# Set attention and a gated feed-forward layer on one core: the product sums of three groups in one PSUM buffer, and the small work around the first attention rearranged

## The chip, the cores and the metric

The kernel runs on one core of one Trainium2 chip. The metric is the device time of one execution in microseconds. Three executions of the kernel before gave 1244.42, 1245.16 and 1248.59 us, so the median is 1245.16 us. A measurement of this kernel can tell a change of about 0.3% (some 3.7 us) from no change.

## What is computed

Four batches of 12608 rows of 128 numbers are attended twice through 32 inducing rows, and every row of the result then goes through a feed-forward layer of width 1024 with a softmax gate and a layer norm:

```python
h  = mab(I, x)            # first attention: 32 inducing rows look at all rows of x
y  = mab(x, h)            # second attention: every row of x looks at the 32 rows h
hh = y @ w_in             # 128 -> 1024
solu = hh * softmax(hh)
ln = (solu - mean) / sqrt(var + 1e-6) * g_ln
out = ln @ w_out          # 1024 -> 128
```

`mab(q, kv)` is softmax(q kv^T / sqrt(128)) kv with the row maximum taken off first.

## The kernel before

**Tiles.** A batch is 99 slots of 128 rows (the last one has 64), in 25 groups of four slots. The kernel folds the second attention into the first matmul of the layer: for each slot, `main` multiplies the slot's 32 attention weights (tile `aT`) by `hs`, a 32 x 1024 product of `h` and `w_in`, in eight small matmuls (L1009). These write one of the four PSUM buffers `h0` to `h3`, each of two PSUM banks. There are 396 such slots.

**One slot's way** (`soft`): VectorE scales and takes the minimum (L1050), ScalarE exponentiates with a sum (L1061), GpSimd multiplies the two (L1065), ScalarE squares with a sum (L1076), VectorE transposes in blocks of 32 (L1089). When the four slots of a group are transposed, `products` starts two streams, w = 0 and w = 1. Each stream accumulates 32 steps in a PSUM buffer of its own (L1132, output 128 x 2 x 129: 128 columns and the sum). `evacuate` copies the buffer to SBUF (L1155), on VectorE or ScalarE. After five groups, `finish` works out mean and variance in a chain of small ScalarE and GpSimd instructions (L1177 to L1191), GpSimd scales each group's rows (L1198), and the rows are stored. There are 100 groups and 20 calls of `finish`.

**Row groups of TensorE.** All these matmuls contract over 32 rows, so four can run side by side, in the four 32-row strips of the array. A stream uses two strips (w = 0 the lower two, w = 1 the upper two), and so does a slot's matmul or a transpose of 32 rows. The helper `beats` writes the order: in one beat it emits a pair of matmuls for each stream that has work, or a pair of a slot's or a transpose's matmuls and a pair of the other stream. A beat with two pairs is called full in this document, one with a single pair half.

**First attention** (`p1`). For batches 1 to 3 it runs beside the layer of the batch before, in groups of up to 16 slots (seven per batch): x is loaded by DMA, transposed on TensorE (L583), copied (L593), stored transposed in DRAM for the second attention, scored against the inducing rows (L643), and the maximum per row of scores is taken on VectorE (L659). Scores lie in four quarters of the partitions, so the four partial maxima have to become one: VectorE spreads them (L663), one small matmul with `fold2` brings them together (L668), VectorE takes the maximum with the running one (L677) and scales it (L684). Then comes the exponential (L694), a transpose (L714), a matmul that gathers the weighted rows of x (L725) in a second visit to a PSUM buffer, and the update of the running sum (L741). Batch 0 does the same in the start of the kernel with PSUM buffers of its own (`early`). `combine` closes a batch (L767 to L793), and `p2` makes the weights of the second attention (L833 to L910).

**What sets the order.** A planner written in Python lists the instructions: each has an engine, a cost, what it comes after, and a priority, and each engine's list is fixed before the launch. The numbers at the top of the file (`EAGER`, `P1_STEP`, `PR_*`, `SLACK`, `WINDOW_TILES`, `MINE`) set priorities and windows. On the chip each engine takes its list in that order and waits on semaphores. `PAIR[w]` lets a stream have one group at a time, `TURN` (of `MINE` tokens) limits slots between L1009 and L1050, and `H` holds the four PSUM buffers. `HN` and `EU` are the buffers of L1050 and L1061.

Of the kernel before, what the change touches and what calls it, by code (L numbers as in the profile page):

```python
# [19 lines left out]
P = 128  # L20
C = 128
# [12 lines left out]
EAGER = 300  # L34
SWITCH = 400

# [19 lines left out]
HN_MORE = 4  # L56
# [6 lines left out]
P1_STEP = 10.5  # L63
# [5 lines left out]
PR_G2 = 8  # L69
PR_HN = -4  # L70
PR_MU = -4
PR_SQ = 4
PR_TU = 12
RUSH = -100.0
SLACK = {"PE": 0, "ACT": 200, "DVE": 100, "POOL": 100, "SP": 0}
SPARE = 150
WARM = 32
WINDOW_TILES = 3
MINE = 2
OP_FIRST = -30  # L80
WOUT = -8
WIN = -18.5
# [8 lines left out]
DMA_LAG = 1800  # L91
# [159 lines left out]
def set_attention_then_solu_kernel(ctx: ExitStack, tc: tile.TileContext, x, inducing, w_in, w_out, g_ln, out):  # L251
# [67 lines left out]
    EW = Lock()  # L319
    ST = Lock([  # L320
# [9 lines left out]
    SM = Lock([small(i, mloc=1, mdiag=4, junk=4, nb=1, fac=1, ls=1, rl=1) for i in range(4)])  # L330
# [200 lines left out]
    turned = [Event() for _ in range(NP[0])]  # L531

    def p1(b, k):
# [9 lines left out]
        halves = [(0, GS), (GS, n)] if early and not k and n > GS else [(0, n)]  # L543
        for c0, c1 in halves:
            for nbytes, fn in move(b, s0 + c0, c1 - c0, xn[:, c0:, :], False):
                d = yield dma(nbytes, fn, rel)
                xd.append((d, c0))
# [21 lines left out]
        def by_rows(ways):  # L569
# [4 lines left out]
            def turn():  # L574
                w = min(ways, key=lambda w: (load(w) > 0, w))
# [9 lines left out]
                beats(-(-n // 2), (1 - w,), two)  # L585

# [35 lines left out]
        def store():  # L622
            def go():
                nc.sync.dma_start(xT_dram[b][:, s0 * P : (s0 + n) * P], xT[:, :n, :].rearrange("p s t -> p (s t)"))

            d = yield dma(n * P * C * 4, go, ready)
            plan.set(xd_done[(b, k)], d)
            plan.set(stored, d)
# [5 lines left out]
        if not early:  # L634
            (eT, ew), erel = yield lew
# [11 lines left out]
        d = yield Op("PE", (0 if early else SWITCH) + n * 60, scores, ready, rel, ind_ready.after)  # L647
# [9 lines left out]
        for lo, hi, nn in parts:  # L657
            d = yield Op(
                "DVE", 411, lambda: nc.vector.tensor_reduce(out=v["mloc"][lo:hi], in_=sc[lo:hi, : nn * M], op=ALU.max, axis=AX.X), dsc  # L659
            )  # L660
        d = yield Op(
            "DVE", 131,
            lambda: nc.vector.tensor_scalar(  # L663
                out=v["mdiag"], in0=quarter, scalar1=v["mloc"], scalar2=None, op0=ALU.mult, op1=ALU.max, accum_out=v["nb"]
            ),
            d,
        )
        d = yield Op("PE", (80 if early else SWITCH) + 110, lambda: nc.tensor.matmul(mq, lhsT=fold2, rhs=v["mdiag"], start=True, stop=True), d)  # L668
# [6 lines left out]
        d = yield Op(  # L675
            "DVE", 122,
            lambda: nc.vector.tensor_scalar(  # L677
                out=v["junk"], in0=mq, scalar1=(-3.0e38 if first else mold), scalar2=None, op0=ALU.max, op1=ALU.max, accum_out=mnew
            ),
            d, prev,  # L680
        )
        plan.set(chain[b][k + 1], d)
        dm = d = yield Op(
            "DVE", 70, lambda: nc.vector.tensor_scalar(out=v["nb"], in0=mnew, scalar1=-scale, scalar2=None, op0=ALU.mult), d  # L684
        )
        df = None
        if early:
            (eT, ew), erel = yield lew
# [9 lines left out]
        de = d = yield Op("ACT", (130 + 35 * n) * len(parts) + (0 if first else 190), exps, dm, erel)  # L698
# [15 lines left out]
        d = yield Op("DVE", 435, lambda: nc.vector.transpose(out=ew[:, :n, :].rearrange("p s m -> p (s m)"), in_=eT[:, : n * M]), d)  # L714
        nq = min(4, n)
        rel = None
        if not early:
            give(lpb, big, de)
            big, rel = yield lpb
        pooled = big[:, 512 - C : 512]  # L720

        def gather():
# [6 lines left out]
        dp = yield Op("PE", 74 * n, gather, d, rel)  # L729
# [20 lines left out]
        give(lpb, big, da)  # L750
# [9 lines left out]
    def combine(b):  # L760
# [11 lines left out]
        d = yield Op("DVE", 200, lambda: nc.vector.tensor_scalar(out=accn, in0=acc, scalar1=rl, scalar2=None, op0=ALU.mult), d, prev)  # L772
# [33 lines left out]
    def p2(b, j):  # L806
# [4 lines left out]
        for k, (g0, gn) in enumerate(p1_groups[b]):  # L811
# [4 lines left out]
        d = yield dma(  # L816
            n * P * C * 4,
            lambda: nc.sync.dma_start(xT[:, :n, :].rearrange("p s t -> p (s t)"), xT_dram[b][:, s0 * P : (s0 + n) * P]),
            rel, prev,
        )  # L820
# [38 lines left out]
        def turned_rows():  # L859
# [4 lines left out]
            def turn():  # L864
                w = min(ways, key=lambda w: (load(w) > 0, w))
# [11 lines left out]
                beats(-(-pairs // 2), (1 - w,), two)  # L877

# [40 lines left out]
    stream = [dict(j=JB, emit=None, ready=0.0, close=None) for _ in range(2)]  # L919
    flow = {"idle": Event(), "left": 2 * NB * NG, "prio": 0.0}  # L920

    def load(w):
        p = stream[w]
        return JB - p["j"] if p["j"] < JB and p["ready"] <= plan.now + EAGER else 0

    def beats(count, pairs=(0, 1), also=None):

        for i in range(count):
            if also:
                also(i)  # L930
            went = False
            for w in pairs:
                p = stream[w]
                if p["j"] < JB and p["ready"] <= plan.now + i * BEAT + EAGER:
                    p["emit"](2 * w, p["j"])
                    p["emit"](2 * w + 1, p["j"])
                    p["j"] += 1
                    went = True
            if not (went or also):
                return i  # L940
        return count
# [374 lines left out]
```

## Time and profile before

| what | value |
|---|---|
| median of three executions | 1245.16 us |
| the profiled execution: its own time | 1244.09 us |
| its span, first to last instruction | 1242.3 us |
| TensorE matmul busy | 1196.1 us (96%) |
| VectorE, ScalarE, GpSimd busy | 1092.8, 1085.6, 1087.8 us |
| mean granted TensorE clock | 0.979 |
| DMA | 113.61 MB, mean 91 GB/s |

Durations below come from this one profiled execution. Matmuls overlap each other, so a busy TensorE is not a full TensorE. A float32 matmul stands in the records twice: 12800 product matmuls are 25600 records. The column after the engines in a table of stages is the granted clock of TensorE, 1.00 being full speed.

### The profile page before, as it was taken

To read this page: it belongs to the slowest core of one execution; us is meant where nothing else is said; L and a number is where in the kernel's file an instruction comes from. 1 tells how busy PE (TensorE), PEld (TensorE's weight loads), DVE (VectorE), ACT (ScalarE), POOL (GpSimd) and SP (SyncE) were. 2 spreads that over 40 slices of the span, in tenths; PEclk is the share of its full clock that TensorE was granted. 3 is DMA by queue.
4 is the path that set the end of the run, shared out by engine and by line. 5 is a ranking of instruction groups with operands and counts; after the bars stand their busy time and mean duration, and the time that the engine had idled before them with its cause. 6 is when DMAs were issued, how large, how long until landed. Compare 5 with 4: busy or idle time off the path is not lost. (4 is left out here: it accounts for less than half of the span.)

```text
span 1242.3 us, 77962 instructions
## 1 busy us (share of the span) xinstructions
PE 1196.1 (96%) x35557; PEld 1112.9 (90%) x35557; DVE 1092.8 (88%) x1684; ACT 1085.6 (87%) x2152; POOL 1087.8 (88%) x638
## 2 busy tenths in 40 slices
PE   9999999999999989999999999999999999999995
PEld 7679999999998988998999899999899999999995
DVE  5689999999897989899988889989899999898982
ACT  5489998999897979898889889999888999998983
POOL 3478898988987878989898898989898999998996
PEclk9969999999999999999999999999999999989998
DMA  9663243321234233331223333523220212112013
GB/s 355 234 166 111 72 135 90 101 68 38 81 90 130 82 102 110 94 104 50 73 56 108 103 112 101 158 57 110 63 54 16 73 48 61 47 19 48 6 47 85
DMA packets 152908, 113.61 MB, mean 91 GB/s; under 512 B 76257, under 2 KB 132609, under 8 KB 148097
## 3 DMA queue, kind: packets, MB, share of 16 engines
q1 hardware_dynamic: 152576, 108.62, 29.2%
q8 instruction: 278, 4.55, 1.6%
q14 instruction: 54, 0.43, 0.1%
HBM read 54.30 MB, written 52.18 MB: 86 GB/s over the span
## 5 line engine op out<-in xcount | busy, mean ns | idle before, releaser
L1132 PE MATMUL h<-wc,vt 32*128 32x129 f32 (+1 forms) x25600 | 1030.4, 275 | 22.4 <-issue 13.7
L1132 PEld LDWEIGHTS h<-wc,vt 32*128 32x128 f32 (+1 forms) x25600 | 992.7, 186 | 60.6 <-issue 38.6
L1065 POOL TENSOR_TENSOR eu<-spare,eu 128x1024 f32<-128x1024 f32 x227 | 535.7, 2376 | 45.3 <-ACT eu L1061 45.0
L1089 DVE STREAM_TRANSPOSE vt<-eu 128x1024 f32<-128x1024 f32 x396 | 481.6, 1230 | 13.5 <-POOL eu L1065 12.9
L1076 ACT ACTIVATE sq<-eu 128x1024 bf16<-128x1024 f32 x396 | 416.7, 1052 | 47.5 <-POOL eu L1065 37.0
L1009 PE MATMUL h<-hs,aT 32*128 32x128 f32 x6336 | 435.2, 276 | 4.1 <-ACT aT L889 1.7
L1065 POOL TENSOR_TENSOR eu<-hn,eu 128x1024 f32<-128x1024 f32 x169 | 399.7, 2377 | 38.9 <-ACT eu L1061 38.7
L1009 PEld LDWEIGHTS h<-hs,aT 32*128 32x128 f32 x6336 | 392.2, 189 | 23.2 <-issue 6.7
L1050 DVE TENSOR_SCALAR_CACHE_REDUCE spare<-h,rn 128x1024 f32<-128x1024 f32 x227 | 285.8, 1265 | 40.4 <-PE h L1009 23.8
L1061 ACT ACTIVATE eu<-spare,nm 128x1024 f32<-128x1024 f32 x227 | 259.1, 1142 | 10.3 <-DVE spare L1050 7.8
L1050 DVE TENSOR_SCALAR_CACHE_REDUCE hn<-h,rn 128x1024 f32<-128x1024 f32 x169 | 212.8, 1264 | 29.9 <-PE h L1009 17.0
L1061 ACT ACTIVATE eu<-hn,nm 128x1024 f32<-128x1024 f32 x169 | 192.9, 1142 | 7.4 <-DVE hn L1050 4.8
L1198 POOL TENSOR_TENSOR spare<-spare,fin 128x512 f32<-128x512 f32 x100 | 101.2, 1044 | 1.4
L1076 ACT ACTIVATION_READ_ACCUMULATOR sq<-eu 128x1 f32 x396 | 74.8, 189 | 0.0
L1155 ACT COPY spare<-h 128x258 f32<-128x258 f32 (+1 forms) x127 | 45.7, 364 | 29.4 <-PE h L1132 28.2
L583 PE MATMUL h<-ident,xn 32*128 32x32 f32 x1188 | 54.1, 225 | 0.3 <-issue 0.3
L583 PEld LDWEIGHTS h<-ident,xn 32*128 32x128 f32 x1188 | 50.4, 136 | 0.7 <-issue 0.5
L593 ACT COPY xT<-h 128x1024 f32<-128x1024 f32 (+2 forms) x42 | 37.8, 901 | 10.1 <-PE h L583 9.8
L1155 DVE COPY spare<-h 128x258 f32<-128x258 f32 (+1 forms) x73 | 30.2, 416 | 18.4 <-PE h L1132 18.0
L1061 ACT ACTIVATION_READ_ACCUMULATOR eu<-spare,nm 128x1 f32 x227 | 43.0, 190 | 0.0
L875 PE MATMUL h<-ident,a 32*128 32x32 f32 (+1 forms) x800 | 34.2, 221 | 1.4 <-ACT a L852 1.1
L889 ACT COPY aT<-h 128x512 f32<-128x512 f32 (+3 forms) x66 | 30.2, 472 | 5.6 <-PE h L875 5.5
(154 smaller groups left out, 655.2 us busy)
## 6 DMA issues: line engine op xcount, KB each, us to landing
out_dram<-spare SPq DMA_DIRECT2D x96, 256.0 KB, 3.7
xT<-xd SPq DMA_DIRECT2D x19, 1024.0 KB, 5.7
xn<-in_x_dram SPq DMA_DIRECT2D x15, 1024.0 KB, 6.3
xd<-xT SPq DMA_DIRECT2D x15, 1024.0 KB, 5.1
dl<-dd SPq DMA_DIRECT2D x396, 1.0 KB, 2.8
xd<-vt SPq DMA_DIRECT2D x7, 768.0 KB, 10.3
spare<-in_x_dram SPq DMA_DIRECT2D x5, 768.0 KB, 12.8
xT<-xd SPq DMA_DIRECT2D x5, 768.0 KB, 5.6
```

Of the source, the lines that this page charges most:

```text
L583: nc.tensor.transpose(out=tr[:, k * 512 + s * M : k * 512 + (s + 1) * M], in_=xn[r, s, :], identity=ident[r, r])
L593: lambda: nc.scalar.copy(xT.rearrange("c s (q t) -> c q s t", q=4)[:, 2 * w : 2 * w + 2, :n, :], tr.rearrange("c (k x) -> c k x", k=2)[:, ...
L875: nc.tensor.transpose(out=tr[:h, k * 512 + q * M : k * 512 + (q + 1) * M], in_=both, identity=ident[r, r])
L1009: nc.tensor.matmul(hp[:, cols], lhsT=aT[rows, i // 2, :], rhs=hs[rows, cols], start=True, stop=True)
L1050: lambda: nc.vector.tensor_scalar(out=hn, in0=hp, scalar1=rn, scalar2=None, op0=ALU.mult, op1=ALU.min, accum_out=nm),
L1061: "ACT", 1133, lambda: nc.scalar.activation(e, hn, AF.Exp, bias=nm, scale=-1.0, accum_out=G["qe"][:, s, 1:2]), d, rel, srel,
L1065: d = yield Op("POOL", 2330, lambda: nc.gpsimd.tensor_tensor(out=e, in0=hn, in1=e, op=ALU.mult), de, prio=t + PR_MU)
L1076: "ACT", 1040, lambda: nc.scalar.activation(sq, e, AF.Square, scale=1.0 / 32.0, accum_out=G["qe"][:, s, 0:1]), d,
L1089: lambda: nc.vector.transpose(out=G["vtb"][:, : n * FF].rearrange("p (j s t) -> p j s t", j=M, s=n)[:, :, s, :], in_=e.rearrange("p (a f) ...
L1132: nc.tensor.matmul(op[:rows, a - 2 * w, : C + 1], lhsT=vt[q, k, :], rhs=wc[q, k, :], start=(k == 0), stop=(k == JB - 1))
L1155: return lambda: eng(F["raw"][:rows, i0 : i0 + 2, :], op[:rows, :, : C + 1])
L1198: return lambda: eng.tensor_tensor(out=raw, in0=raw, in1=y[:, i0 : i0 + 4].unsqueeze(2).to_broadcast([rows, 4, C]), op=ALU.mult)
```

## The change

It has five parts and new numbers for the planner.

1. **Three groups in one buffer.** The groups of a `finish` are taken by three (and two): the sums of group 1, 2 and 3 of a stream lie side by side in one PSUM buffer, at columns 0, 129 and 258 of each bank. The buffer is taken at the first and evacuated once, after the last, by one copy of 2 x 3 x 129. A stream is now a queue: a group may stand ready behind the one that runs.
2. **Attention's sums with the next scores.** For batches 1 to 3 the gather of group k goes out together with the scores of group k + 1 and writes a free part of the same PSUM buffer. Only the last group of a batch has a visit of its own.
3. **No folded maxima.** For batches 1 to 3 the small matmul L668 goes; VectorE moves the four partial maxima together and spreads the result with small 32 x 1 instructions, and ScalarE scales it.
4. **Rows scaled by two engines.** The scaling of a group's rows may go to ScalarE, as four instructions of 128 x 128, instead of GpSimd.
5. **x moves whole.** A load or store may be cut in pieces of `PIECE` slots with at most `TOKENS` under way; with 16 the groups of up to 16 slots go in one piece.

`beats` also tells the planner what it took, with a surcharge for going from half to full.

```diff
-EAGER = 300
+EAGER = 0
+OS_ACT = 1
+SLOTS = 3
+PIECE = 16
+TURN_ON = 90
-HN_MORE = 4
+HN_MORE = 3
-P1_STEP = 10.5
+P1_STEP = 12
-SLACK = {"PE": 0, "ACT": 200, "DVE": 100, "POOL": 100, "SP": 0}
+SLACK = {"PE": 0, "ACT": 400, "DVE": 200, "POOL": 100, "SP": 0}
-WINDOW_TILES = 3
-MINE = 2
+WINDOW_TILES = 1
+MINE = 3
...
 def p1(b, k):
...
+        def visit():
+            scores()
+            if before:
+                gathers[(b, k - 1)](big[:, 512 + P : 512 + P + C])
...
+            def near():
+                for g in range(1, 4):
+                    same(v["quart"][quad[0], g : g + 1], v["quart"][quad[g], 0:1])
...
+            dm = d = yield Op("ACT", 135, lambda: nc.scalar.activation(v["nb"], mnew, AF.Copy, scale=-scale), d)
...
 def products(b, j, t, w):
...
-        bank, rel = yield H.at(OP_FIRST + t)
-        op = bank.rearrange("p (k x) -> p k x", k=2)
+        slot, last = slot_of[j]
+        if slot == 0:
+            held[w] = yield H.at(OP_FIRST + t)
+            held[w] += ([],)
+        bank, rel, mine = held[w]
+        mine.append(j)
+        op = bank.rearrange("p (k x) -> p k x", k=2)[:, :, slot * (C + 1) : (slot + 1) * (C + 1)]
...
-            spawn(evacuate(b, j, w, op, bank, d, t + PR_EV), t + PR_EV)
-            give(PAIR[w], None)
+            if last:
+                spawn(evacuate(b, mine, w, bank, d, t + PR_EV), t + PR_EV)
+                give(PAIR[w], None)
+        stream[w].append(dict(j=0, emit=emit, ready=ready, close=close, prio=t + PR_G2))
+        if not last:
             give(PAIR[w], None)
...
 def finish(b, f):
...
-            done = yield Op("POOL", 1000, scaled(nc.gpsimd), dy, prio=OS_PRIO)
+            def each_quarter():
+                for a in range(4):
+                    act(raw[:, a, :], raw[:, a, :], AF.Copy, scale=y[:, i0 + a : i0 + a + 1])
+
+            done = yield Op("POOL", 1000, scaled(nc.gpsimd), dy, prio=OS_PRIO, alt=Op("ACT", 1010, each_quarter, dy, prio=OS_PRIO) if OS_ACT else None)
```

**What moves on TensorE, at the end of a group.** Before, about slot 311: stream 0 (buffer h0) and stream 1 (h3) alternate in pairs; names are output buffer <- inputs, `x2` is the number of matmuls in a row.

```order
L1132 MATMUL h3_697<-wc_151,vt_65 96x129 x2
L1132 MATMUL h0_694<-wc_151,vt_65 128x129 x2
L1132 MATMUL h3_697<-wc_151,vt_65 96x129 x2
L1132 MATMUL h0_694<-wc_151,vt_65 128x129 x14
L1132 MATMUL h1_695<-wc_151,vt_65 128x129 x2
L1132 MATMUL h0_694<-wc_151,vt_65 128x129 x2
```

The group in h3 ends, and h0 goes on alone for 14 matmuls, of which six or seven pairs are half beats, until the next group starts in another buffer, h1. In the change, the same place in the life of a group (its 64 matmuls of a stream end just ahead of the L1115 row, and the next group's begin behind it):

```order
L1244 MATMUL h2_651<-wc_151,vt_65 128x129 x2
L1244 MATMUL h1_650<-wc_151,vt_65 128x129 x2
L1115 MATMUL h3_652<-hs1_119,aT1_96 128x128 x8
L1244 MATMUL h2_651<-wc_151,vt_65 128x129 x2
L1244 MATMUL h1_650<-wc_151,vt_65 128x129 x2
L1244 MATMUL h2_651<-wc_151,vt_65 128x129 x2
```

Both streams go on in the buffers they had, h2 and h1, with no stretch of one alone; a slot's eight matmuls (L1115, was L1009) stand between.

**What moves on TensorE, in the first attention.** Before, the gather L725 is a visit of its own, in buffer h3, between product matmuls:

```order
L1132 MATMUL h2_696<-wc_151,vt_65 128x129 x2
L1132 MATMUL h1_695<-wc_151,vt_65 128x129 x8
L725 MATMUL h3_697<-xn0_67,ew_99 32x128 x16
L1132 MATMUL h1_695<-wc_151,vt_65 128x129 x2
L1132 MATMUL h2_696<-wc_151,vt_65 128x129 x2
```

In the change it (L784) stands right behind the next group's scores (L668, was L643), in the same buffer, and the matmul of the maxima is gone:

```order
L1244 MATMUL h3_652<-wc_151,vt_65 128x129 x4
L1244 MATMUL h1_650<-wc_151,vt_65 128x129 x2
L668 MATMUL h2_651<-xT_85,indT_150 32x512 x4
L784 MATMUL h2_651<-xn1_68,ew_99 32x128 x16
L1115 MATMUL h0_649<-hs1_119,aT1_96 128x128 x2
L1244 MATMUL h1_650<-wc_151,vt_65 128x129 x2
```

**What moves on ScalarE.** Before, the last small step of a `finish` (L1190) is followed by the usual exponentials (L1061) and squares (L1076):

```order
L1061 ACTIVATE eu,qe_106<-spare,nm_112 128x1024
L1190 ACTIVATE fin_109<-fin_109 128x20
L1061 ACTIVATE eu,qe_106<-spare,nm_113 128x1024
L1076 ACTIVATE sq,qe_104<-eu 128x1024
L1076 ACTIVATE sq,qe_106<-eu 128x1024
```

In the change, the rows of two groups are scaled there, eight instructions (L1322) ahead of the next square (L1183, was L1076); exponentials are L1168 now:

```order
L1310 ACTIVATE fin_109<-fin_109 128x20
L1183 ACTIVATE sq,qe_100<-eu 128x1024
L1168 ACTIVATE eu,qe_102<-spare,nm_112 128x1024
L1168 ACTIVATE eu,qe_102<-hn_81,nm_113 128x1024
L1322 ACTIVATE spare<-spare,fin_109 128x128 x8
L1183 ACTIVATE sq,qe_100<-spare 128x1024
```

Each of the 20 calls of `finish` has eight such instructions on ScalarE, in one run or in two of four, and three scalings left on GpSimd.

Counted over the whole program: L668 on TensorE falls from 30 instructions to 9 (those of batch 0), GpSimd's scalings from 100 to 60, and ScalarE gets 160 of 128 x 128 and 21 of 128 x 1. The 200 evacuations become 88 (16 of one group, 32 of two, 40 of three). DMA instructions are the same in number and size. In the order of TensorE, beats number 4435 before (4037 full; 398 half, of which 299 are a product's and 99 a slot's) and 4347 in the change (4102 full; 245 half, of which 144 are a product's), with the half beats of transposes left out of both (506 and 529).

## The prediction on record

> **What bounds the kernel now.** I read the page first, then the table of stages, then short stretches of TensorE alone, then the waits.
>
> ```profile
> span 1242.3 us, 77962 instructions
> PE 1196.1 (96%) x35557; PEld 1112.9 (90%) x35557; DVE 1092.8 (88%) x1684; ACT 1085.6 (87%) x2152; POOL 1087.8 (88%) x638
> ```
>
> Four engines are nearly equally busy, and the share of busy time doesn't tell which one leads. So I cut the span where the work changes: the start, the stretch with a first attention beside the layer (85 to 900 us), the last batch without one (900 to 1212 us), and the end. The columns are the stage, its length, busy time and instructions of PE, PEld, DVE, ACT and POOL, then the granted clock. The two rows behind it are the slots' matmuls alone (L1009, 16 records for each slot).
>
> ```profile
> 0.00:85.00 85.00, 78.49 (x931) 60.84 (x931) 57.24 (x149) 53.39 (x116) 41.74 (x38) 0.86 0.78 265
> 85.00:900.00 815.00, 796.26 (x24426) 738.87 (x24425) 741.80 (x1142) 734.98 (x1444) 724.29 (x412) 1.00 0.31 93
> 900.00:1212.00 312.00, 305.03 (x9647) 297.24 (x9642) 287.66 (x387) 287.32 (x567) 302.26 (x168) 0.98 0.17 42
> 1212.00:1243.00 31.00, 16.29 (x576) 15.91 (x570) 6.14 (x7) 9.94 (x27) 19.46 (x22) 0.81 0.32 85
> ...
> 85.00:900.00 815.00, 299.78 (x4364) 269.38 (x4366) 1.00 0.31 93
> 900.00:1212.00 312.00, 122.23 (x1832) 111.13 (x1828) 0.98 0.17 42
> ```
>
> The middle makes 4364 / 16 = 273 slots in 815 us, 2.99 us each, and the late stage 114.5 in 312 us, 2.72 us each. In the late stage GpSimd leads with 302.3 of 312 us (97%). In the middle GpSimd, ScalarE and VectorE are at 89 to 91% and TensorE's matmuls at 98%. Is TensorE full there, or only covered by overlapping records? Four half microseconds of TensorE alone answer it:
>
> ```profile
> 1006.00:1006.50 0.50, 0.50 (x28) 1.00 0.15 2
> 1006.50:1007.00 0.50, 0.50 (x28) 1.00 0.15 2
> 1014.00:1014.50 0.50, 0.50 (x14) 1.00 0.45 115
> 1014.50:1015.00 0.50, 0.50 (x13) 1.00 0.82 328
> ```
>
> All read as 100% busy, but the first two touch 28 records and the last two 13 or 14: with one stream alone, half as many matmuls go by in the same time. So a half beat costs what a full one does. The price of a beat stands in the final run, where both streams go on undisturbed:
>
> ```profile
> 1214.06 14.58 PE h L1132 x512
> ```
>
> 512 records are 256 matmuls or 64 full beats: 0.228 us each. Of the 4435 beats some 3010 lie in the middle (counted in the order between slots 12 and 280): 686 us. The first attention's and p2's scores and gathers (some 60 visits of about 1.1 us), 406 half beats of 32-column transposes at 0.06 to 0.1 and the small matmuls add about 100. That is nearly all of the 815 us, so TensorE leads in the middle.
>
> One rule of the Trainium skill reads this otherwise: "Perfetto Trace Analysis", section "Identifying the Most-Contended Engine", wants TensorE judged by the busy share of its weight loads, not of its matmuls. By it TensorE has 738.9 of 815 us, 90.7%, no more than VectorE's 91.0%, and beats saved on TensorE would bring nothing in the middle: of the sum below only the other stages' 4.5 us would be left, 1241 (a rival, with its chance below). The count of records per half microsecond speaks against it here: the weight loads thin out with the half beats, and the beats take as long.
>
> **The change, part by part.** *Fuller beats.* Between slots 12 and 280 beats fall from 3010 to 2971: 39 x 0.228 = 8.9 us off TensorE in the middle; behind slot 280 from 1353 to 1332, 4.8 us, where GpSimd leads and hides nearly all of it.
>
> *No folded maxima.* The matmul with its neighbours, in order of time:
>
> ```profile
> 505.56 0.99 PE L1132 MATMUL h<-wc,vt 32*128 32x129 f32 x16
> 506.48 0.38 PE L668 MATMUL h<-small,fold 128*128 128x4 f32 x2
> 506.79 2.17 PE L1132 MATMUL h<-wc,vt 32*128 32x129 f32 x66
> ```
>
> The products end at 506.55 and begin again at 506.79, and the ones ahead took 0.99 us for two full beats. So it costs TensorE between 0.24 and 0.6; I take 0.4, near its own duration: 21 x 0.4 = 8.4 us, in the middle. In its place VectorE gets 126 instructions of 32 x 1 and 21 of 32 x 4 and loses 63 small ones, 21 each of the rows below: 21 x (199 + 206 + 134) = 11.3 us. At the smallest of these, 134 ns, the new 147 are 19.7 us, so this costs VectorE up to 8 us more, or saves up to 11 if they hide behind longer ones. I take nothing: VectorE isn't the leader. The longer chain delays only the exponential of a group that has some 36 us.
>
> ```profile
> L663 DVE TENSOR_SCALAR_CACHE_REDUCE small<-quarter,small 128x4 f32<-128x4 f32 x30 | 6.0, 199 | 0.4
> L677 DVE TENSOR_SCALAR_CACHE_REDUCE small<-h,m 128x4 f32<-128x4 f32 x18 | 3.7, 206 | 0.2
> L684 DVE TENSOR_SCALAR small<-m 128x1 f32<-128x1 f32 x30 | 4.0, 134 | 0.3
> ```
>
> *Gathers beside the scores.* The matmuls stay; 18 visits to another buffer go. A visit's cost beyond its matmuls lies between 0 and the 0.24 us above: I take 0.1, 2 us. The x tile is held until the next scores, and the next load waits for that; the load is short beside 36 us:
>
> ```profile
> xn<-in_x_dram SPq DMA_DIRECT2D x15, 1024.0 KB, 6.3
> ```
>
> *Evacuations.* The nearest rows, one group against whole copies:
>
> ```profile
> L1155 ACT COPY spare<-h 128x258 f32<-128x258 f32 (+1 forms) x127 | 45.7, 364 | 29.4 <-PE h L1132 28.2
> L1155 DVE COPY spare<-h 128x258 f32<-128x258 f32 (+1 forms) x73 | 30.2, 416 | 18.4 <-PE h L1132 18.0
> L889 ACT COPY aT<-h 128x512 f32<-128x512 f32 (+3 forms) x66 | 30.2, 472 | 5.6 <-PE h L875 5.5
> L593 ACT COPY xT<-h 128x1024 f32<-128x1024 f32 (+2 forms) x42 | 37.8, 901 | 10.1 <-PE h L583 9.8
> ```
>
> Two groups (516 columns) then take about 0.47 on ScalarE and three (774) about 0.7. With 10, 22 and 30 of one, two and three groups that is 35 us against 45.7; VectorE, with a dearer column, gets about 19 for 30.2. Each saves 11 us, three quarters of it in the middle.
>
> *Scaling by two engines.* GpSimd's 1044 ns leave 40 times, at the pitch of a run of five, 5.04 us:
>
> ```profile
> 1021.49 5.04 POOL L1198 TENSOR_TENSOR spare<-spare,fin 128x512 f32<-128x512 f32 x5
> 49.85 0.70 ACT L460 ACTIVATE hn<-hn,g_sb 128x128 f32<-128x128 f32 x2
> L460 ACT ACTIVATE hn<-hn,g_sb 128x128 f32<-128x128 f32 x8 | 2.9, 393 | 0.0
> ```
>
> So GpSimd loses 40 us. ScalarE's nearest row is the scaling of w_out by g, the same form: 393 ns alone, two in a row 0.70, so 0.31 for each further one. 160 x 0.31 = 50 us, not the 40 that the planner's 1010 for four says. ScalarE's net is 50 + 4 (the 21 small ones at 0.2) - 11 = +43 us.
>
> *DMA, buffers and the planner's numbers.* The DMA list is the same in sizes and number, so x moving whole changes nothing. HN has six buffers instead of seven and EU six instead of five: bounds 0 to a few us, within the stage terms. I take 0 for the start (same work; up to 3 us either way).
>
> **The sum.** Middle: TensorE's 796.3 falls by 8.9 + 8.4 + 2 less 1 for 14 more transposes, to 778; ScalarE's 735 rises by 69% of 43 (273 of 396 slots) to 765, VectorE's falls to 734, GpSimd's to 697. TensorE still leads. At its present fill (796.3 / 815 = 0.977) the stage would be 796, 19 less; ScalarE would then be at 96%, about as full as GpSimd is where it leads today (97%), so I let it stand; it is the weakest term. Late: GpSimd 302.3 - 11.7 = 291, ScalarE 287.3 + 12.4 = 300; at the fill that GpSimd has there (0.969) 300 makes 309.5: 2.5 less. End: five scalings in a row are the last work, and with two of them on ScalarE 2 us go:
>
> ```profile
> 1232.01 5.03 POOL L1198 TENSOR_TENSOR spare<-spare,fin 128x512 f32<-128x512 f32 x5
> ```
>
> Together 19 + 2.5 + 2 = 23.5. The profiled execution took 1244.1 us (span 1242.3, 1.8 around it) and lies 1.1 below the median, so the forecast is 1244.1 - 23.5 + 1.1, rounded **1222 us**. Its own range: 1232 if only half of the middle's 19 comes, 1212 if half of the tightening below comes too.
>
> **The rivals.** The waits that speak for and against them:
>
> ```profile
> POOL eu L1065 <- ACT eu L1061: 83.7, 54, 6.3
> DVE spare L1050 <- PE h L1009: 23.8, 30, 5.1
> PEld h L1132 <- ACT spare L1155: 5.1, 14, 0.8
> PEld h L1132 <- DVE spare L1155: 3.3, 5, 0.8
> ```
>
> *Everything tightens.* Waits between the engines go with the half beats: GpSimd idles 83.7 us for exponentials and VectorE 23.8 for slots' matmuls, both fed by TensorE. If the middle comes to 785 (TensorE at 99%, 30 less), the late stage to 304 (8 less) and the end gives 3, the time is 1204. A sixth buffer EU speaks for it, a ScalarE at 97% against it.
>
> *The pinned buffers starve TensorE (slower).* Two of four PSUM buffers are held for three groups; at each of the 88 turnovers a stream needs a new one. If none is free, TensorE waits for the longer evacuation: 0.7 to 0.95 us and some 0.5 of semaphores, 1.3 us; both streams turn near each other, so 44 x 1.3 = 57 us against the 23.5: 1279, and from 18 such waits on nothing is gained. A rule of the Trainium skill stands behind this: "Perfetto Trace Analysis", section "Matmuls" (under "Optimizing Tensor Performance"), wants independent groups to rotate through different banks, so that one's evacuation overlaps the next one's matmuls. The trace says that today, with 200 turnovers, TensorE's loads waited 8.4 us in all for evacuations, and the order still turns over into another buffer.
>
> *ScalarE's bursts (slower).* Eight scalings are 2.5 us in front of an exponential; GpSimd takes 2.38 a slot, so with less than one slot waiting the burst passes through to it. 20 x 2.5 = 50 would eat the gain from the tenth on; 16 of them, 40 us, make 1262. For it: the 83.7 us. Against it: GpSimd has 40 us less to do.
>
> *TensorE isn't the leader (no change).* If VectorE and ScalarE, at 91% and 90% with their waits for each other, set the middle, only 4.5 us come: 1241, which a measurement can hardly tell. The bare shares speak for it, the 3010 beats of 0.228 against it.
>
> *The clock (no change).* When TensorE waits, its clock halves for some 6 us:
>
> ```profile
> 1112.00:1118.00 6.00, 6.00 (x98) 0.50 0.00 0
> ```
>
> Such a spell costs 3 us. The late stage, where TensorE doesn't lead, has about three in 312 us; at that rate a middle that ScalarE leads would get eight more, 24 us, and the time would stay at 1246.
>
> **Chances.** Forecast 0.61; tightening 0.15; pinned buffers 0.08; bursts 0.06; TensorE not the leader 0.05; clock 0.05. Faster by over 0.3% (below 1241.4): 0.61 + 0.15 = 0.76. Within 0.3%, what a measurement can tell: 0.05 + 0.05 = 0.10. Slower: 0.14. The range 1200 to 1246 takes in the forecast, the tightening a little past its own figure, and the two of no change, and leaves out the slower cases.
>
> **What would show it.** Right: between the start and the last attention a slot takes about 2.92 us, ScalarE is at 94% or more there, GpSimd's wait for exponentials falls, and no wait for an evacuation stands among the ten longest. The 160 scalings take about 0.31 us each in a run. Wrong: idle time of TensorE ahead of the products (L1244) put down to evacuations (L1272), more stretches at half clock, or a middle as long as before with ScalarE the fullest engine.

## The result, and the profile after

The changed kernel takes 1239.4 us in the median of 14 runs (1231.6 to 1247.55), the kernel before 1245.24 in the 14 beside them (1239.41 to 1250.37): ratio 0.9944, 95% interval 0.9919 to 0.9968. It is faster by 7 us (4 to 10). The forecast was 23.5 us: the direction and the range hold, its size is over three times what came.

The profiled execution took 1235.15 us. The span and the busy time from its page:

```profile
span 1233.3 us, 77892 instructions
PE 1164.7 (94%) x35487; PEld 1084.1 (88%) x35487; DVE 1094.5 (89%) x1693; ACT 1122.0 (91%) x2272; POOL 1049.8 (85%) x601
```

TensorE's busy time fell by 1196.1 - 1164.7 = 31.4 us, but the span only by 1242.3 - 1233.3 = 9.0. The difference is TensorE's idle time: 46.2 us before, 68.6 now. The stages of the changed kernel (stage, length, busy time and instructions of PE, PEld, DVE, ACT, POOL, then the clock; the late stage's cut lies at 1200 here), then the slots' matmuls alone (L1115) and the products alone (L1244) in the middle and the late stage:

```profile
0.00:85.00 85.00, 76.19 (x927) 59.80 (x930) 61.38 (x160) 56.17 (x123) 43.10 (x38) 0.86 0.77 265
85.00:900.00 815.00, 780.56 (x24607) 729.28 (x24606) 743.91 (x1156) 761.16 (x1522) 703.87 (x390) 0.99 0.31 90
900.00:1200.00 300.00, 288.32 (x9282) 275.68 (x9280) 280.17 (x371) 286.97 (x581) 284.44 (x157) 1.00 0.20 49
1200.00:1234.00 34.00, 19.59 (x696) 19.37 (x688) 9.02 (x9) 17.72 (x49) 18.35 (x19) 0.83 0.29 78
```

```profile
85.00:900.00 815.00, 301.74 (x4326) 267.66 (x4326) 0.99 0.31 90
900.00:1200.00 300.00, 121.55 (x1792) 109.08 (x1792) 1.00 0.20 49
```

```profile
85.00:900.00 815.00, 706.73 (x17695) 680.68 (x17694) 0.99 0.31 90
900.00:1200.00 300.00, 271.87 (x7206) 263.17 (x7204) 1.00 0.20 49
```

The same row of the kernel before, products in the middle:

```profile
85.00:900.00 815.00, 717.21 (x17404) 685.65 (x17405) 1.00 0.31 93
```

By slots alone the middle is no faster: 4326 records are 270.4 slots, 3.01 us each, against 2.99. But a slot's matmul and its products need not fall into the same stage, so count both: 4326 + 17695 = 22021 records against 4364 + 17404 = 21768. The middle did 253 records more in the same 815 us, 1.2%, 9.5 us. Of the 31936 records of the whole run 9948 are left at 900 us before, for 342.3 us, and 9669 now, for 333.3: 29.1 and 29.0 per us. So the profiled gain of 9 us lies in the middle, and the late stage and the end add nothing.

TensorE's longest waits, before and after (who waited, for whom, us in total, times, longest):

```profile
PE h L1132 <- issue: 13.7, 12, 2.7
PE h L1132 <- DVE vt L1089: 4.0, 4, 1.7
...
PE h L875 <- ACT a L852: 1.1, 2, 0.8
PE h L1009 <- issue: 1.1, 2, 0.7
...
PE h L1009 <- DVE spare L1050: 0.8, 2, 0.6
PE h L1132 <- ACT spare L1155: 0.7, 3, 0.4
...
PE h L1132 <- DVE spare L1050: 0.5, 1, 0.5
...
PE h L1132 <- DVE hn L1050: 0.3, 1, 0.3
```

```profile
PE h L1244 <- issue: 16.9, 19, 2.9
PE h L1115 <- issue: 11.3, 8, 2.9
PE h L961 <- ACT a L938: 5.7, 6, 1.3
PE h L1244 <- ACT spare L1272: 4.2, 8, 1.7
...
PE h L1115 <- DVE spare L1157: 2.1, 3, 1.5
PE h L1115 <- DVE hn L1157: 2.0, 6, 0.7
PE h L1244 <- DVE hn L1157: 1.4, 3, 0.6
PE h L1244 <- DVE spare L1157: 1.4, 2, 1.0
...
PE h L1244 <- DVE spare L1272: 1.3, 3, 0.7
```

"issue" is time in which the profile shows nothing to wait for: ahead of slots and products 14.8 us before, 28.2 after. The transposes of the second attention's weights (L875, now L961) waited 1.1 us for ScalarE's exponential, now 5.7. Waits for an evacuation (L1155, now L1272) went from 0.7 to 4.2 + 1.3 = 5.5 us, waits for VectorE's scaling of a slot, which frees a PSUM buffer (L1050, now L1157), from 1.6 to 6.9. GpSimd's waits for exponentials did not fall, as the forecast wanted, but grew from 83.7 us:

```profile
POOL eu L1172 <- ACT eu L1168: 95.7, 78, 4.9
...
POOL spare L1172 <- ACT spare L1168: 13.0, 15, 2.6
```

### The profile page after: what moved, and what is told of

Read it like the earlier page. It is cut to its first block, busy times and chain, and to the rows that moved or that the text cites. A ratio compares the mean times of both kernels' runs of the same rounds, so it can differ in the third digit from the quotient of the medians.

```text
span 1233.3 us, 77892 instructions
## 1 busy us (share of the span) xinstructions
PE 1164.7 (94%) x35487; PEld 1084.1 (88%) x35487; DVE 1094.5 (89%) x1693; ACT 1122.0 (91%) x2272; POOL 1049.8 (85%) x601
## 5 line engine op out<-in xcount | busy, mean ns | idle before, releaser
L1244 PE MATMUL h<-wc,vt 32*128 32x129 f32 x25600 | 1001.1, 274 | 29.0 <-issue 16.9
L1244 PEld LDWEIGHTS h<-wc,vt 32*128 32x128 f32 x25600 | 965.8, 185 | 53.4 <-issue 32.9
L1172 POOL TENSOR_TENSOR eu<-hn,eu 128x1024 f32<-128x1024 f32 x197 | 464.3, 2375 | 46.2 <-ACT eu L1168 44.8
L1115 PE MATMUL h<-hs,aT 32*128 32x128 f32 x6336 | 440.5, 277 | 17.2 <-issue 11.3
L1115 PEld LDWEIGHTS h<-hs,aT 32*128 32x128 f32 x6336 | 392.2, 189 | 41.0 <-issue 12.2
L1196 DVE STREAM_TRANSPOSE vt<-eu 128x1024 f32<-128x1024 f32 x330 | 401.5, 1228 | 6.8 <-POOL eu L1172 6.2
L1172 POOL TENSOR_TENSOR eu<-spare,eu 128x1024 f32<-128x1024 f32 x133 | 314.5, 2376 | 54.5 <-ACT eu L1168 50.9
L1183 ACT ACTIVATE sq<-eu 128x1024 bf16<-128x1024 f32 x330 | 346.1, 1049 | 7.1 <-POOL eu L1172 3.6
L1157 DVE TENSOR_SCALAR_CACHE_REDUCE hn<-h,rn 128x1024 f32<-128x1024 f32 x198 | 248.8, 1261 | 40.4 <-PE h L1115 19.2
L1157 DVE TENSOR_SCALAR_CACHE_REDUCE spare<-h,rn 128x1024 f32<-128x1024 f32 x198 | 249.0, 1263 | 33.2 <-PE h L1115 18.6
L1168 ACT ACTIVATE eu<-hn,nm 128x1024 f32<-128x1024 f32 x197 | 224.4, 1140 | 1.3 <-DVE vt L1196 1.3
L1172 POOL TENSOR_TENSOR spare<-spare 128x1024 f32<-128x1024 f32 x65 | 154.4, 2375 | 12.4 <-ACT spare L1168 12.2
L1168 ACT ACTIVATE eu<-spare,nm 128x1024 f32<-128x1024 f32 x133 | 151.5, 1140 | 1.2 <-DVE vt L1196 0.6
L1196 DVE STREAM_TRANSPOSE vt<-spare 128x1024 f32<-128x1024 f32 x66 | 80.8, 1224 | 0.0
L1168 ACT ACTIVATE spare<-spare,nm 128x1024 f32<-128x1024 f32 x65 | 74.0, 1139 | 0.2 <-DVE spare L1157 0.2
L1183 ACT ACTIVATE sq<-spare 128x1024 bf16<-128x1024 f32 x66 | 69.3, 1050 | 1.8 <-POOL spare L1172 0.8
L1183 ACT ACTIVATION_READ_ACCUMULATOR sq<-eu 128x1 f32 x330 | 62.8, 190 | 0.0
L1272 ACT COPY spare<-h 128x774 f32<-128x774 f32 (+3 forms) x62 | 40.5, 655 | 17.7 <-PE h L1244 12.5
```

The costliest lines, as they stand in the source:

```text
L1115: nc.tensor.matmul(hp[:, cols], lhsT=aT[rows, i // 2, :], rhs=hs[rows, cols], start=True, stop=True)
L1157: lambda: nc.vector.tensor_scalar(out=hn, in0=hp, scalar1=rn, scalar2=None, op0=ALU.mult, op1=ALU.min, accum_out=nm),
L1168: "ACT", 1133, lambda: nc.scalar.activation(e, hn, AF.Exp, bias=nm, scale=-1.0, accum_out=G["qe"][:, s, 1:2]), d, rel, srel,
L1172: d = yield Op("POOL", 2330, lambda: nc.gpsimd.tensor_tensor(out=e, in0=hn, in1=e, op=ALU.mult), de, prio=t + PR_MU)
L1183: "ACT", 1040, lambda: nc.scalar.activation(sq, e, AF.Square, scale=1.0 / 32.0, accum_out=G["qe"][:, s, 0:1]), d,
L1196: lambda: nc.vector.transpose(out=G["vtb"][:, : n * FF].rearrange("p (j s t) -> p j s t", j=M, s=n)[:, :, s, :], in_=e.rearrange("p (a f) ...
```

## The experiments

Two theories stood at the start. The forecast's: TensorE sets the middle's pace, so what it saves comes. The rival: the pace is shared, each engine in its fixed order waits in turn for another, and no engine's saving comes whole. A second rival had ScalarE, 36 us fuller, as the new bound. Ratios are to the kernel before, timed beside each; differences to the changed kernel are taken through its 0.9944. The intervals are 3 to 7 us wide to either side, so a difference of a few us between two runs says little.

### One engine lighter, the order kept: the changed kernel

Each run takes work from one engine, and the order of the engines' work stays. Two of them also add something: a_pool and b_pool have 186 and 143 more semaphore instructions on GpSimd ahead of the multiplication.

a_pe, narrower product matmuls:

```diff
-nc.tensor.matmul(op[:rows, a - 2 * w, :], lhsT=vt[q, k, :], rhs=wc[q, k, :], start=(k == 0), stop=(k == JB - 1))
+nc.tensor.matmul(op[:rows, a - 2 * w, 13:], lhsT=vt[q, k, :], rhs=wc[q, k, 13:], start=(k == 0), stop=(k == JB - 1))
```

> The changed kernel, its order kept, with the product matmuls on 116 columns instead of 129 (the first 13 output columns aren't computed): TensorE loses 13/129 of 0.228 us on some 2763 beats that hold products alone, about 63 us; no other engine changes. Shared pace (no engine leads, each waits for the others in turn): 10 to 30 us come, about 1210 to 1230. TensorE leads, as the forecast said: about 50 come, 1190. ScalarE leads since the change: under 8 come, 1232 to 1240.

0.9916 (0.9881 to 0.9950), 3 us under the changed kernel, whose 0.9944 the interval holds. But the edit missed its purpose, as the last run of products shows, of the changed kernel and then of a_pe:

```profile
1195.75 23.84 PE L1244 MATMUL h<-wc,vt 32*128 32x129 f32 x812
```

```profile
1195.78 21.27 PE L1244 MATMUL h<-wc,vt 32*128 32x116 f32 x728
```

29.4 ns for each record at 129 columns, 29.2 at 116: a tenth fewer columns make a beat no shorter. (The weight loads of these matmuls kept their 128 columns; whether they set the length of a beat was not tried.) So a_pe took nothing off TensorE and says nothing on who leads. The next run takes whole beats away instead.

a_skip, every tenth beat of two products left out:

```diff
-                    p["emit"](2 * w, p["j"])
-                    p["emit"](2 * w + 1, p["j"])
+                    skip or p["emit"](2 * w, p["j"])
+                    skip or p["emit"](2 * w + 1, p["j"])
```

(skip is true at each tenth beat in which both streams have a step other than a group's first or last and nothing else goes by.)

> The changed kernel, the order of everything else kept, with every tenth beat left out in which both streams put in products and nothing else goes by (197 beats of 0.224 us; those steps' products aren't summed): TensorE loses 44 us, no other engine changes. TensorE sets the middle's pace, as the forecast said: 35 or more come, about 1204. Shared pace (each engine waits in turn for another, so what one saves comes back in part): 8 to 18 come, 1221 to 1231. ScalarE sets it since the change: under 5 come, 1234 or more.

0.9748 (0.9712 to 0.9785): 24 us under the changed kernel, of the 44 taken away (197 beats of 0.224 us, an estimate), between the two theories. In the changed kernel TensorE leads, but only a little over half of what it saves comes.

a_act, a_pool and a_dve, narrower squares, multiplications and transposes:

```diff
-"ACT", 1040, lambda: nc.scalar.activation(sq, e, AF.Square, scale=1.0 / 32.0, accum_out=G["qe"][:, s, 0:1]), d,
+"ACT", 1040, lambda: nc.scalar.activation(sq[:, :864], e[:, :864], AF.Square, scale=1.0 / 32.0, accum_out=G["qe"][:, s, 0:1]), d,
```

```diff
-nc.gpsimd.tensor_tensor(out=e, in0=hn, in1=e, op=ALU.mult)
+nc.gpsimd.tensor_tensor(out=e[:, :960], in0=hn[:, :960], in1=e[:, :960], op=ALU.mult)
```

```diff
+na = 28 if (G["vt_id"], s) in seen else M
+seen.add((G["vt_id"], s))
...
-                out=G["vtb"][:, : n * FF].rearrange("p (j s t) -> p j s t", j=M, s=n)[:, :, s, :],
-                in_=e.rearrange("p (a f) -> p a f", f=M),
+                out=G["vtb"][:, : n * FF].rearrange("p (j s t) -> p j s t", j=M, s=n)[:, :na, s, :],
+                in_=e[:, : na * M].rearrange("p (a f) -> p a f", f=M),
```

> The changed kernel, its order kept, with the squares on 864 of 1024 columns (the rest isn't summed): ScalarE loses 160 columns of about 0.95 ns on 396 slots, 60 us. Shared pace: 10 to 30 us come, 1210 to 1230. ScalarE leads since the change: about 45 come, 1195. TensorE leads: under 8 come.

> The changed kernel, its order kept, with the multiplication on 960 of 1024 columns (the last 64 keep the exponential): GpSimd loses 64 columns of 2.3 ns on 396 slots, 59 us. Shared pace: 10 to 30 us come, 1210 to 1230. TensorE or ScalarE leads: under 5 come, since GpSimd has 110 us of slack in the middle and about 16 in the late stage.

> The changed kernel, its order kept, with the transpose on 896 of 1024 columns (the other blocks keep an earlier group's values): VectorE loses 128 columns of about 1.15 ns on some 390 slots, 57 us. Shared pace: 10 to 30 us come, 1210 to 1230. TensorE or ScalarE leads: under 5 come.

a_act 0.9860 (0.9802 to 0.9918), 10 us under the changed kernel; a_pool 0.9954 (0.9913 to 0.9994), 1 us above; a_dve 0.9905 (0.9874 to 0.9935), 5 under. The edits took less than was expected: by the pages' busy time 46 us off ScalarE (60 expected), 53 off GpSimd (59) and 43 off VectorE (57). ScalarE isn't the bound either: 46 us give 10, with an interval of 3 to 18.

### The same on the kernel before

b_skip, b_pool, b_act and b_dve make the same four edits in the kernel before.

> The kernel before with the same edit: 182 beats, 41 us of TensorE. TensorE sets the middle's pace there, on which the forecast rested: 30 or more come, ratio 0.976 or less. Shared pace: 8 to 15 come, ratio about 0.990. TensorE isn't a leader: under 4 come, ratio over 0.997.

> The kernel before, its order kept, with the multiplication on 960 of 1024 columns (the last 64 keep the exponential): GpSimd loses 59 us. GpSimd sets the pace of the kernel before, and the change helped by taking 40 us of scalings from it: 20 us or more come, ratio under 0.984. Some other engine sets it: under 6, ratio over 0.995. Shared between GpSimd and ScalarE: 8 to 15.

> The kernel before, its order kept, with the squares on 864 of 1024 columns (the rest isn't summed): ScalarE loses 60 us. ScalarE sets the pace of the kernel before: 20 us or more, ratio under 0.984. GpSimd sets it: under 6, ratio over 0.995. Shared between the two: 8 to 15.

> The kernel before, its order kept, with the transpose on 896 of 1024 columns (the other blocks keep an earlier group's values): VectorE loses 57 us. VectorE sets the pace: 20 us or more, ratio under 0.984. GpSimd or ScalarE sets it: under 6, ratio over 0.995. If neither this run nor the two others bring 6 us, no engine's work sets the pace, but the order and the waits that it holds.

The us taken are the fall of the engine's busy time from page to page; for TensorE, whose records overlap, they are an estimate, 182 beats of 0.224 us.

| taken off | us taken | ratio | 95% interval | us gained |
|---|---|---|---|---|
| TensorE (b_skip) | 41 | 0.9974 | 0.9949 to 0.9998 | 3 |
| GpSimd (b_pool) | 53 | 0.9958 | 0.9933 to 0.9982 | 5 |
| ScalarE (b_act) | 48 | 0.9962 | 0.9936 to 0.9988 | 5 |
| VectorE (b_dve) | 42 | 0.9982 | 0.9954 to 1.0009 | 2 |

This is what decides on the forecast. TensorE, 98% busy in the middle, had 41 us taken from it, and 3 came. No engine alone sets the pace of the kernel before. Where the 41 us went can be followed in b_skip's profile:

```profile
span 1245.9 us, 75050 instructions
PE 1182.5 (95%) x34101; PEld 1090.4 (88%) x34101; DVE 1092.0 (88%) x1684; ACT 1084.8 (87%) x2152; POOL 1087.8 (87%) x638
```

TensorE's idle time rose from 46.2 to 63.4 us, 17 of the 41. Overlapping records hide the rest, so count the distances from one matmul's start to the next in both traces: those under 0.15 us at full clock fell from 1009 to 958 us in all, the longer ones at full clock rose from 176 to 210, and stretches at half clock from 42 to 63. What was saved in the beats came back as pauses and as slower clock. The clock is a small part of it: the three executions of b_skip at a granted clock of 0.977 took 1239.1 to 1240.4 us, the two of the kernel before beside them at that clock 1243.9 and 1246.9, so at the same clock some 6 of the 41 us come (an estimate).

The chain of work that ended last in b_skip goes through all of them:

```profile
by line: POOL eu L1065 25.9%; PE h L1132 23.4%; PE h L1009 9.0%; issue 7.3%; ACT sq L1076 4.9%; POOL spare L1198 4.4%; ACT eu L1061 3.7%; DVE vt L1089 2.1%; DVE spare L1050 1.8%; DVE hn L1050 1.3%; PE h L833 0.9%; PE h L583 0.9%; PE h L725 
```

### Savings together

b_three has the edits of GpSimd, ScalarE and VectorE in one kernel, b_all TensorE's as well.

> The same without TensorE's part: GpSimd -59, ScalarE -60, VectorE -57 us. TensorE binds together with one of the others before, right behind it: 4 to 10 come, ratio 0.992 to 0.997, and the four savings together far more. The three others bind among themselves, and TensorE has room: 20 or more, ratio under 0.984.

> The kernel before, its order kept, with all four savings at once: every tenth product beat left out, multiplication on 960, squares on 864 and transpose on 896 of 1024 columns (TensorE -41, GpSimd -59, ScalarE -60, VectorE -57 us; what is left out isn't computed). Several engines bind at once: 35 us or more come, ratio under 0.972. The order's waits and fixed latencies set the pace: 15 or less, ratio over 0.988.

b_three 0.9870 (0.9828 to 0.9913), 16 us (11 to 21) where the three alone add up to 12; b_all 0.9741 (0.9716 to 0.9766), 32 us. TensorE's 41 us, worth 3 alone, are worth 32 - 16 = 16 when the others are lighter too. So TensorE binds together with the others. But even all four at once, with at least 41 us off each, bring 32. That the rest of the pace is waits between the engines that don't shrink with the work is argued from this, not shown.

### One part alone

b_os gives the kernel before only the second engine for the row scaling; os0 takes that away from the changed kernel; slots1 gives each group its own buffer again.

```diff
-done = yield Op("POOL", 1000, scaled(nc.gpsimd), dy, prio=OS_PRIO)
+done = yield Op("POOL", 1000, scaled(nc.gpsimd), dy, prio=OS_PRIO, alt=Op("ACT", 1010, each_quarter, dy, prio=OS_PRIO))
```

```diff
-OS_ACT = 1
+OS_ACT = 0
```

```diff
-SLOTS = 3
+SLOTS = 1
```

> The kernel before with ScalarE as a second engine for the row scaling and nothing else of the change, the order planned anew (192 instructions of ScalarE, 60 us, for 48 of GpSimd, 50 us). GpSimd sets the pace before: faster, 1225 to 1235. The parts only pay together: no change, 1240 to 1250. ScalarE at 91% before has no room: slower, 1250 to 1262.

> The changed kernel with all 100 row scalings on GpSimd, and the order planned anew: ScalarE loses 62 us, GpSimd gains 41. If ScalarE's load is what ate the gain: 10 or more come in the middle, and GpSimd at 97% of the late stage gives some 5 back: about 1232. If GpSimd is as near the limit: no change or slower, 1239 to 1248.

> The changed kernel with a buffer for each group, as before the change (200 evacuations instead of 88), the order planned anew: TensorE gets back some 40 to 90 half-filled beats (10 to 20 us), ScalarE and VectorE about 11 us each. TensorE sets the pace: 1249 to 1259. Shared pace: 3 to 8 slower, 1242 to 1247. Pinned buffers cost what the sharing saves: the same or faster, 1235 to 1240.

b_os 1.0095 (1.0066 to 1.0125), 12 us slower than the kernel before; os0 1.0126 (1.0091 to 1.0162) and slots1 1.0084 (1.0052 to 1.0116), 23 and 17 us slower than the changed kernel. Read straight, each part is worth more than the whole and one of them is harmful alone. But each of these kernels also has a new order on every engine, so the next question was what a new order costs by itself.

### Another order of the same work

b_n1 and a_n1 change one of the planner's cost figures by one per cent, b_n2 and a_n2 another. No instruction is added or taken away on purpose; the planner, with a slightly different idea of time, lays out another order.

```diff
-"ACT", 1040, lambda: nc.scalar.activation(sq, e, AF.Square, scale=1.0 / 32.0, accum_out=G["qe"][:, s, 0:1]), d,
+"ACT", 1050, lambda: nc.scalar.activation(sq, e, AF.Square, scale=1.0 / 32.0, accum_out=G["qe"][:, s, 0:1]), d,
```

```diff
-d = yield Op("POOL", 2330, lambda: nc.gpsimd.tensor_tensor(out=e, in0=hn, in1=e, op=ALU.mult), de, prio=t + PR_MU)
+d = yield Op("POOL", 2340, lambda: nc.gpsimd.tensor_tensor(out=e, in0=hn, in1=e, op=ALU.mult), de, prio=t + PR_MU)
```

> The kernel before with one cost figure of the planner moved by one per cent (a square at 1050 ns for 1040) and nothing else: the same instructions in another order, 4949 beats with the transposes' where the kernel before has 4941. The time follows from the loads: 1243 to 1248, ratio 0.998 to 1.002. The order's waits set it, and the kernel before is a lucky one of many plans: slower by 5 to 25, ratio 1.004 to 1.020.

> The changed kernel with the same one figure moved (a square at 1050 ns): 4896 beats where it has 4876, else the same work. The time follows from the loads: 1238 to 1246. The order's waits set it: 1245 to 1262, slower than the changed kernel by more than its gain.

> The kernel before with another figure of the planner moved (the multiplication at 2340 ns for 2330) and nothing else: the same work, 4945 beats with the transposes' for 4941. The order's waits set the time: again slower than the kernel before, ratio 1.004 to 1.015. Loads set it, and the first pair was bad luck: 0.998 to 1.002.

> The changed kernel with the same figure moved (2340 ns): 4874 beats for 4876. If the change by itself is worth some 0.3 to 0.6%, as the two pairs so far say: 0.3 to 0.6% under the nudged kernel before, ratio 1.000 to 1.011. If it is worth the forecast's 1.9%, and the two pairs hid it: 1.4% or more under it. If it is worth nothing: equal to it within 0.3%.

| planner's figures | before | changed | changed to before |
|---|---|---|---|
| as they are | 1 | 0.9944 (0.9919 to 0.9968) | 0.9944 |
| square 1050 | 1.0078 (1.0046 to 1.0110) | 1.0053 (1.0021 to 1.0085) | 1.0053 / 1.0078 = 0.9975 |
| multiplication 2340 | 1.0134 (1.0097 to 1.0171) | 0.9978 (0.9953 to 1.0004) | 0.9978 / 1.0134 = 0.9846 |

The page of b_n1:

```profile
span 1256.1 us, 77942 instructions
PE 1195.6 (95%) x35557; PEld 1109.1 (88%) x35557; DVE 1100.6 (88%) x1707; ACT 1081.9 (86%) x2133; POOL 1085.7 (86%) x634
```

Its busy times are those of the kernel before to within 8 us on every engine (TensorE 1195.6 for 1196.1), and its span is 13.8 us longer: all of it idle time. In the four kernels a figure moved costs 10, 17, 14 and 4 us, in three of them more than the change brought. The work is nearly the same: the planner also moves some copies from ScalarE to VectorE (19 in b_n1), and in a_n1 TensorE is busy for 15 us more than in the changed kernel (1180.1). The three ratios have a mean of 0.992: over these three orders the change is worth about 10 us, with single orders between 3 and 19; each of the two new ratios is uncertain by some 0.0045 (an estimate from the two intervals behind it). The last, 1.5%, is not far from the forecast's 1.9%, but the loads don't tell which pair of orders has it. That also takes the edge off the section above: b_os, 1.0095, lies between the two nudged kernels before, so its part alone costs nothing that an order doesn't; os0 and slots1, 1.0183 and 1.0141 of the changed kernel, lie above its two nudged plans (1.0110 and 1.0034), which one order each doesn't settle. No kernel with the whole computation beat the changed one.

## Why the forecast was wrong, point by point

**What the engines save and get: right, but for VectorE.** TensorE was to come down to 778 us in the middle; it has 780.6. ScalarE was to rise to 765; it has 761.2. The 160 scalings were put at 0.31 us each in a run; a run of eight in the changed kernel:

```profile
1173.00 2.44 ACT L1322 ACTIVATE spare<-spare,fin 128x128 f32<-128x128 f32 x8
```

With 0.39 for the last that is (2.44 - 0.39) / 7 = 0.29 for each further one. GpSimd's total fell by 38.0 us (40 foreseen). VectorE's total rose by 1.7 where evacuations were to bring it down by 11: the small instructions for the maxima, put at nothing, ate that (126 of them on one line, L710, take 18.2 us). In the middle VectorE has 743.9 us, not 734.

**A half beat costs a full one: the traces agree.** In the trace of the kernel before the two records of one stream alone, at 1014 us, follow the last two by 0.111 us, and the four of both streams, at 1220 us, the last four by 0.112. a_pe agrees: a beat has a length of its own, which a tenth fewer columns don't change.

**"TensorE leads in the middle", and with it "at its present fill the stage would be 796, 19 less": this step failed.** It was called the weakest term, for ScalarE's sake, but it failed before the change already: the kernel before gives 3 us for 41 taken from TensorE. Its 98% busy was read as the bound. The beats are full-priced indeed, but time taken off them does not come off the stage whole. Of the middle's 19 us about 9.5 came. The fill, which the sum held at 0.977, fell to 780.6 / 815 = 0.958. The trace says where to: more "issue", later buffers, as listed above. That TensorE's saving comes back as pauses and slower clock is shown by b_skip. That the order, fixed on all engines, makes TensorE wait for its neighbours a little later is the likely reading, and that these particular waits grew because of the change is only read from the trace. The 9.5 us that are missing in the middle are also no more than an order alone can cost, so the share of each stays open.

**Late stage 2.5 less, end 2 less: nothing came.** The forecast had GpSimd lead there with 302.3 of 312 us; its own table has TensorE's matmuls at 305.0, 98% as in the middle, and it passed over that. GpSimd's busy share in the late stage fell from 97% to 284.4 / 300 = 95%. But TensorE (288.3) and ScalarE (287.0) stand at 96% there, and the rate of 29.0 records per us is that of before.

**Start, 0: right.** Up to 85 us the two lines have 246 records where there were 220, less than 1 us of work at that rate.

**The signs that it named.** The scalings came at their price. But a slot of the middle takes 3.01 us, not 2.92, ScalarE stands at 761.2 / 815 = 93.4%, not 94 or more, and GpSimd waits longer for exponentials, not less. Of the signs against it, one came: an evacuation (L1272) ahead of L1244 stands fourth among TensorE's waits.

**The rivals.** *TensorE isn't the leader*, 1241 us, is 1.6 us from the result, and had a chance of 0.05. The rule beside it, the Trainium skill's in "Perfetto Trace Analysis", section "Identifying the Most-Contended Engine", judged TensorE by its weight loads, 90.7% in the middle and no more than VectorE. For the kernel before b_skip agrees with it. The prediction's reason against it, that weight loads thin out with the half beats, holds for their count alone: in the half microsecond from 1014.00 they are busy for 0.50 us of 0.50, as the matmuls are. In the changed kernel that share is lower still, 729.3 / 815 = 89.5%, and there 44 us off TensorE bring 24, so the share alone doesn't tell. And the place was wrong: that rival had the gain in the other stages, and it came in the middle. *The pinned buffers* show in a small form, the waits above for L1272 and L1157, about 10 us more than before, and not the 57 of that rival. Its 0.5 us for semaphores at each turnover is too much: of the 22 matmuls and weight loads of products that waited for L1155 in the kernel before, 16 start within 0.08 us of the copy's end. *ScalarE's bursts* could lie behind GpSimd's longer waits for exponentials. At a_act's rate, 10 us for 46, ScalarE's 36 us more cost some 8, an estimate. *Tightening* and *the clock* did not come: the mean granted clock is 0.979 before and 0.980 after. Between executions of one kernel the time goes with the clock, though: of the 14 of the changed kernel the fastest, 1231.6 us, has 0.987 and the slowest, 1247.55, has 0.976. Which of the two is the cause was not tried.

**What was missing among the rivals** is that the order itself is a quantity. With all loads as computed, a new order moves this kernel by up to 17 us. The forecast's own range of 1212 to 1232 had no term for that.

**What stays open.** How much of the 7 us is the change and how much its order: three orders say 3 to 19. What makes one order better than another was not found, nor why 44 us off TensorE bring 24 in the changed kernel and 41 bring 3 in the one before; each saving was tried on one order alone.

## What to carry to other kernels

Where four engines stand at 87 to 96%, a busy share, even 98% of a stage, names no bound; take a known amount off one engine with the order kept, and see what comes, before pricing a change by that engine. When a change makes a planner lay out a new order, the loads don't tell what that order costs: nudge a planner's figure that means nothing, in both kernels, and use that spread as the error of the forecast and of the result. Where a saving doesn't show in the span, look for it in the idle time of the engine that saved: subtract busy time from span, before and after, and then ask what the new idle time waits for.

## What the runs showed of the hardware

A row-tiled product on 116 columns instead of 129 takes as long (29.2 and 29.4 ns per record, 0.23 us for the eight records of a full beat), with weight loads of 128 columns in both.

Most of TensorE's "issue" waits end at a fixed distance behind a landing of instructions. Two records of the changed kernel in order of time, with nothing between them on TensorE and the idle time in brackets:

```profile
681.81 1.07 PE L1244 MATMUL h<-wc,vt 32*128 32x129 f32 x32
685.79 0.98 PE L1244 MATMUL h<-wc,vt 32*128 32x129 f32 x20 [2.91 <-issue]
```

In the trace's DMA records a 16 KB packet of the busier instruction queue (q8) lands 1.37 us ahead of 685.79, and in the stalls of over 1 us that follow one, 5.5 to 9 us (once 16) rather than the median of 3.8 to 3.9 lie between the start of such a packet and that of the one before. Counting TensorE's idle stretches over 0.25 us between 85 and 1215 us that end 1.26 to 1.52 us behind such a landing gives 13, together 13.5 us, in the kernel before, and 21, together 25.8, in the changed one. Of the 11 and 22 stretches among TensorE's that are put down to "issue", 10 and 20 end in that window, which is 0.26 us wide. In the nudged kernels these stretches make 14.0 and 21.4 us before, 27.8 and 23.9 with the change. So the two pairs with the figures as they are and with the square have 12 and 14 us more with the change, the third only 2.5, and an order alone moves it by up to 8. No run took this wait away, so what it costs the span was not tried.
